# Both heads of an attention unit in one operation, and the state readout on four quarters of the TensorE array

## The chip, the cores and the metric

The kernel runs on one core of a Trainium2 chip. The metric is device time of one execution in microseconds (us); lower is better. The core has five engines with a queue each: TensorE (PE, matrix products; its weight loads are listed as PEld), VectorE (DVE), ScalarE (ACT), GpSimd (POOL) and SyncE (SP, which here only issues DMAs). PSUM, where TensorE writes, has eight banks; each holds 512 fp32 values in each of 128 partitions.

## The reference

Three layers follow each other. The first is a gated linear attention with a state, for 4 batches x 8 heads, 768 steps and 48 channels:

```python
for t in range(S):
    state = alpha[:, :, t, :, None] * state + np.einsum('bhd,bhe->bhde', k[:, :, t], v[:, :, t])
    y[:, :, t] = np.einsum('bhd,bhde->bhe', q[:, :, t], state)
```

The heads' outputs are put side by side to 3072 tokens of 384 channels. The second layer is `h = x @ w_in; g = h - tanh(h); x = g @ w_out` with 2048 hidden channels. The third routes each token to one of eight experts (the largest of eight logits) and weighs the expert's output by the softmax value and by a sigmoid output gate.

## The kernel before, in words

Tokens are worked in 8 blocks (`j`) of 384. The attention of one block is 4 units (`p`), each with two heads: head 0 in partitions 0 to 47, head 1 in partitions 64 to 111. So there are 32 units `u`. A unit's 384 steps are cut into `NC` = 6 chunks of `CH` = 64. For each unit the kernel

- scans the decays on DVE (`prep_k`, `prep_q1`) and scales keys and queries with them (`kh`, `kt`, and `prep_q2` for the queries: head 0 into `XA` on DVE, head 1 into `XB` on POOL);
- turns the keys (`turn_k`, TensorE transposes into a bank, `ktok` copied out by ACT) and computes each chunk's contribution to the state (`update`, after `carry` has put the state of the block before in front); a DVE scan, `chain`, makes of it the states `SS` at the start of all chunks, stored as 48 columns x 7 values, so that the states of one chunk lie 7 values (28 bytes) apart;
- multiplies keys and queries within a chunk (`score`) and masks the result (`causal`: one operation for each head's half, on DVE; in units 4 to 7, `CAU`, the second half goes by an ACT copy and a POOL product);
- copies the states on ACT (`states`) beside the values, so that `WA` has head 0's states in partitions 0 to 47 and its values in partitions 64 to 127, and `WB` the reverse for head 1; in the same way `XA` and `XB` have scaled queries and masked scores one below the other;
- reads out (`readout`): for each chunk one product over all 128 partitions for each head, head 0 to output partitions 0 to 63 and head 1 to 64 to 127, side by side in the array;
- copies the result (`y`, a high part by ACT and a low part by DVE in `place`) and lays it out by DMA as `xT`, the input of the second layer: 10 DMAs a block.

The second layer works in fp32r with high and low parts: each of 16 steps `f` of a block has 9 products into a bank of `psh` (`h_step`, first layer), `tanh` on ACT, subtraction on DVE, the high part `gg` by ACT and the low part by DVE or, in block 0, POOL; then 9 products into three accumulator banks `psx` (`x_step`, one step behind). An accumulator has 384 output columns and 16 router columns of its 512. In block 0 each step also narrows and splits the weights (`conv`: DVE L308 to L312, ACT copies, POOL subtractions) and runs `gate(f)`: three transposes of the step's output weights, a copy `wT` by ACT, products with the router weights, `ohi` by ACT and `olo` by DVE. Transposes and products of `gate` use one bank of `psa`.

The PSUM banks are: `psx` three, `psh` two, `psa` three. `psa` serves transposes of keys, state updates, scores, readouts, `gate` and the ranks of the router. In the first four units, before block 0, the `psx` banks help out (`bank`, `early`).

The order of the work: the first four units run ahead of block 0, in an order written out by hand. After that, a unit takes four steps of the second layer: scores, `carry` and `update` in the first, `chain` and `states` in the second, `readout` and `place` in the third, `turn_k` of the next unit in the fourth. In block 0 the order on DVE and SP is written by hand, and the other engines' order is planned from a time model; in blocks 1 to 6 the planner orders all, SP from block 2 on; the last block and the experts (third layer, from some 595 us on) are by hand again. Units end with block 6.

Of the kernel before, what the change touches and what calls it, by code (L numbers as in the profile page):

```python
# [9 lines left out]
F32 = mybir.dt.float32  # L10
# [26 lines left out]
CAU = (4, 5, 6, 7)  # L37
# [27 lines left out]
def tile_kernel(ctx, tc, aps, outs):  # L65
# [23 lines left out]
    psa = pss.enter_context(tc.tile_pool(name="psa", bufs=3, space=PSUM))  # L89
# [30 lines left out]
    XA = [ap1.tile([128, TB], F32, name=f"XA{i}") for i in range(2)]  # L120
    XB = [ap1.tile([128, TB], F32, name=f"XB{i}") for i in range(2)]
    WW = NC * D + 16
    WA = [ap1.tile([128, WW], F32, name=f"WA{i}") for i in range(2)]
    WB = [ap1.tile([128, WW], F32, name=f"WB{i}") for i in range(2)]
    GE = [ap1.tile([128, D, NC + 1], F32, name=f"GE{i}") for i in range(2)]
    VZ = [ap1.tile([128, NA, 2, 2 * D], F32, name=f"VZ{i}") for i in range(2)]
    SS = [ap1.tile([128, D, NC + 1], F32, name=f"SS{i}") for i in range(NP)]
# [64 lines left out]
    def prep_q2(u):  # L192
        s = st[u]
        q, Pc = s["raw"][:, TB:2 * TB], s["Pc"]
        yield dve.tensor_tensor(out=c3(XA[u % 2])[0:D], in0=c3(q)[0:D], in1=Pc[0:D, :, 1:CH + 1], op=ALU.mult)  # L195
        pool.tensor_tensor(out=c3(XB[u % 2])[64:64 + D], in0=c3(q)[64:64 + D], in1=Pc[64:64 + D, :, 1:CH + 1], op=ALU.mult)  # L196
# [19 lines left out]
    def score(u):  # L216
        s = st[u]
        s["sc"] = ps = bank("pss")
        for c in range(NC):
            cs = slice(c * CH, (c + 1) * CH)  # L220
            pe.matmul(ps[64:128, cs], s["kt"][0:D, c], XA[u % 2][0:D, cs], start=True, stop=True)  # L221
            pe.matmul(ps[0:64, cs], s["kt"][64:64 + D, c], XB[u % 2][64:64 + D, cs], start=True, stop=True)

    def causal(u):
        ps = st[u].pop("sc")
        for X, p0 in ((XA, 64), (XB, 0)):
            if p0 == 0 and u in CAU:
                act.copy(X[u % 2][p0:p0 + 64], ps[p0:p0 + 64, 0:TB])
                pool.tensor_tensor(out=c3(X[u % 2][p0:p0 + 64]), in0=c3(X[u % 2][p0:p0 + 64]),
                                   in1=cmask[p0:p0 + 64].unsqueeze(1).to_broadcast([64, NC, CH]), op=ALU.mult)  # L230
                continue
            yield dve.tensor_tensor(
                out=c3(X[u % 2][p0:p0 + 64]), in0=c3(ps[p0:p0 + 64, 0:TB]),
                in1=cmask[p0:p0 + 64].unsqueeze(1).to_broadcast([64, NC, CH]), op=ALU.mult)

    def carry(u):
# [5 lines left out]
        else:  # L242
            act.copy(pu[:, 0:n * D:n], SS[p][:, :, NC])
# [11 lines left out]
    def chain(u):  # L255
        yield dve.tensor_tensor_scan(  # L256
            out=SS[units[u][1]].rearrange("p d c -> p (d c)"), data0=GE[u % 2].rearrange("p d c -> p (d c)"),
            data1=st[u].pop("pu")[:, 0:(NC + 1) * D], initial=0.0, op0=ALU.mult, op1=ALU.add)
# [847 lines left out]
```

## Time and profile before

| | |
|---|---|
| median of 3 runs | 847.51 us (846.33 to 848.63) |
| profiled execution | 847.61 us, span 845.8 us |
| TensorE busy | 807.6 us (95%) |
| VectorE busy | 510.2 us (60%) |
| ScalarE busy | 384.3 us (45%) |
| GpSimd busy | 242.7 us (29%) |
| mean granted TensorE clock | 0.977 |

The span runs from the first to the last instruction of the profiled execution. Busy times are sums over the span. Products are pipelined, so a busy TensorE isn't one at its peak; what an engine waited for is inferred from semaphore events. The granted clock is TensorE's, as a share of 2.4 GHz.

### The profile page before, as it was taken

The numbers are of one execution on the slowest core, as the hardware profiler recorded it, in microseconds if no ns is written. First come the engines' busy times: TensorE is split into PE (matmuls) and PEld (weight loads), VectorE is DVE, ScalarE is ACT, GpSimd is POOL, SyncE is SP. The second block draws the span as 40 slices with busy tenths as digits, with TensorE's granted clock in tenths as the row PEclk, the third lists the DMA queues.
The fourth block names the chain that finished last, engine by engine and source line by source line (L and its number), as shares of the span: only waits on it lengthen the run. The fifth ranks groups of instructions, "written<-read, shape, count | busy, mean of one in ns | idle before, by whom it ended". The sixth has DMA issues, their size and how long they took to land.

```text
span 845.8 us, 15740 instructions
## 1 busy us (share of the span) xinstructions
PE 807.6 (95%) x5968; PEld 753.2 (89%) x5968; DVE 510.2 (60%) x1064; ACT 384.3 (45%) x803; POOL 242.7 (29%) x216
## 2 busy tenths in 40 slices
PE   6689889999999999999999999999999999999995
PEld 4578878999999989999999899999899999999995
DVE  8997989766766665766766664445443434434421
ACT  3555545544444445545443543435343434445431
POOL 6266766121211211120121020012223314424321
PEclk8799999999999999999999999999999999999998
DMA  9556552774322332232242221024345336235400
GB/s 253 156 179 199 170 162 57 232 245 104 90 61 70 94 92 58 76 116 65 64 127 64 58 69 24 15 98 126 130 147 202 103 116 217 96 109 205 156 25 30
DMA packets 59750, 98.48 MB, mean 116 GB/s; under 512 B 19724, under 2 KB 46113, under 8 KB 59665
## 3 DMA queue, kind: packets, MB, share of 16 engines
q1 hardware_dynamic: 56256, 87.91, 34.7%
q0 software_dynamic: 3408, 9.47, 2.9%
q8 instruction: 49, 0.80, 0.4%
q14 instruction: 37, 0.30, 0.1%
HBM read 72.13 MB, written 16.25 MB: 104 GB/s over the span
## 4 chain that ended last, share of the span: by engine, by line
PE 53%; DVE 19%; DMA 9%; issue 8%; ACT 6%; SPq 3%; POOL 2%; POOLq 0%; DVEq 0%; ACTq 0%
PE x L389 13%; PE psh L367 12%; PE o L861 11%; PE psf L833 10%; DMA raw<-raw 7%; DVE Ex L174 3%; DVE t L375 2%; DVE gg L378 2%; SPq L298 2%; DVE w L310 2%; DVE XA L195 2%; DVE w L308 1%; DVE SS L256 1%; PE pss L221 1%; ACT gg L377 1%
## 5 line engine op out<-in xcount | busy, mean ns | idle before, releaser
L389 PE MATMUL x<-ohi,gg 128*128 128x400 f32 x768 | 221.4, 357 | 4.8 <-POOL gg L378 1.3
L367 PE MATMUL psh<-xT,whi 128*128 128x384 f32 x768 | 204.6, 347 | 0.0
L389 PEld LDWEIGHTS x<-ohi,gg 128*128 128x128 f32 x768 | 138.6, 189 | 13.8 <-DVE gg L378 4.3
L367 PEld LDWEIGHTS psh<-xT,whi 128*128 128x128 f32 x768 | 139.7, 192 | 1.1 <-issue 0.3
L389 PE MATMUL x<-olo,gg 128*128 128x400 f32 x384 | 132.4, 345 | 0.0
L367 PE MATMUL psh<-xT,wlo 128*128 128x384 f32 x384 | 131.5, 342 | 0.0
L861 PE MATMUL o<-hi,hh 128*128 128x384 f32 (+2 forms) x440 | 115.1, 338 | 0.0
L375 DVE TENSOR_TENSOR t<-psh,t 128x384 f32<-128x384 f32 x128 | 70.5, 550 | 73.9 <-ACT t L373 73.1
L833 PE MATMUL psf<-xe,hi 128*128 128x256 f32 (+6 forms) x432 | 109.4, 338 | 0.0
L377 ACT CAST gg<-t 128x384 fp32r<-128x384 f32 x128 | 65.7, 513 | 78.6 <-DVE t L375 77.7
L373 ACT ACTIVATE t<-psh 128x384 f32<-128x384 f32 x128 | 62.2, 486 | 82.0 <-PE psh L367 81.2
L839 DVE SCALAR_TENSOR_TENSOR hh<-psf,hh 128x384 fp32r<-128x384 f32 (+3 forms) x96 | 40.9, 447 | 89.9 <-ACT hh L837 89.6
L378 DVE TENSOR_TENSOR gg<-t,gg 128x384 fp32r<-128x384 f32 x114 | 63.6, 557 | 36.0 <-ACT gg L377 35.6
L196 POOL TENSOR_TENSOR XB<-raw,P 48x384 f32<-48x384 f32 x32 | 34.5, 1079 | 160.8 <-issue 119.6
L861 PEld LDWEIGHTS o<-hi,hh 128*128 128x128 f32 (+2 forms) x440 | 78.2, 184 | 1.3 <-DVE hh L839 0.2
L833 PEld LDWEIGHTS psf<-xe,hi 128*128 128x128 f32 x432 | 75.8, 188 | 2.7 <-issue 0.3
L861 PE MATMUL o<-lo,hh 128*128 128x384 f32 (+1 forms) x232 | 77.7, 337 | 0.0
L837 ACT ACTIVATE hh<-psf 128x256 fp32r<-128x256 f32 (+6 forms) x72 | 34.9, 484 | 93.1 <-PE psf L833 75.2
L768 POOL TENSOR_TENSOR lo<-s,hi 128x768 fp32r<-128x768 f32 (+1 forms) x24 | 48.9, 2039 | 94.8 <-ACT hi L767 94.1
L367 PEld LDWEIGHTS psh<-xT,wlo 128*128 128x128 f32 x384 | 73.8, 192 | 0.0
L389 PEld LDWEIGHTS x<-olo,gg 128*128 128x128 f32 x384 | 72.4, 189 | 0.0
L833 PE MATMUL psf<-xe,lo 128*128 128x256 f32 (+6 forms) x216 | 71.9, 333 | 0.0
(147 smaller groups left out, 1274.6 us busy)
## 6 DMA issues: line engine op xcount, KB each, us to landing
raw<-raw SPq DMA_DIRECT2D x32, 579.5 KB, 4.1
wst<-wio SPq DMA_DIRECT2D x32, 384.0 KB, 4.0
s<-w SPq DMA_DIRECT2D x24, 512.0 KB, 4.1
s<-w SPq DMA_DIRECT2D x32, 384.0 KB, 5.1
xT<-y SPq DMA_DIRECT2D x48, 144.0 KB, 2.8
rows<-blank SPq DMA_DIRECT2D x8, 772.0 KB, 6.3
VZ<-vn SPq DMA_DIRECT2D x60, 72.0 KB, 2.4
xs<-rows SPq DMA_DIRECT2D x4, 772.0 KB, 7.3
```

Of the source, the lines that this page charges most:

```text
L196: pool.tensor_tensor(out=c3(XB[u % 2])[64:64 + D], in0=c3(q)[64:64 + D], in1=Pc[64:64 + D, :, 1:CH + 1], op=ALU.mult)
L367: pe.matmul(begun[f][:, 0:TB], w[:, kc, fs], xT[j][:, x, kc], start=(kc + n == 0), stop=(kc == KC - 1 and n == 2))
L373: act.activation(out=t, in_=ps[:, 0:TB], func=AF.Tanh)
L375: dve.tensor_tensor(out=g, in0=ps[:, 0:TB], in1=t, op=ALU.subtract)
L377: act.copy(gg[:, 0], g)
L378: (pool if j == 0 and f not in GLD else dve).tensor_tensor(out=gg[:, 1], in0=g, in1=gg[:, 0].bitcast(F32), op=ALU.subtract)
L389: pe.matmul(px[j][a][:, 0:DG], gg[:, gi, a * 128:(a + 1) * 128], w[:, f], start=(f == 0 and n == 0), stop=(f == NF - 1 and n == 2))
L768: (dve, pool)[i % 2].tensor_tensor(out=lo, in0=t, in1=hi.bitcast(F32), op=ALU.subtract)
L833: pe.matmul(ps[:, 0:n], w[:, kc, fs], xe[:, x, kc], start=(i == 0), stop=(i == 3 * KC - 1))
L837: act.activation(out=hh[:, 0:n], in_=ps[:, 0:n], func=AF.Relu)
L839: dve.scalar_tensor_tensor(out=hh[:, o:o + c.stop - c.start], in0=ps[:, c], scalar=0.0, in1=hh[:, c].bitcast(F32), op0=ALU.max, op1=ALU.su ...
L861: pe.matmul(po[q][m][0:p.stop - p.start, 0:DM], hh[:, p], w[:, f], start=(f == 0 and i == 0), stop=(f == NFE - 1 and i == len(parts) - 1))
```

## The change

- The query product, the mask and the scores are one operation for both heads: `X0` holds both heads' scaled queries, `X1` both heads' masked scores (rows 0 to 63 and 64 to 127). `XB` on POOL goes, and so does the split of `causal` (`CAU`).
- `states` goes: `readout` takes the states straight from `SS` as weights, 48 rows, one value in seven. The values have a tile of their own, `WV`, loaded by one DMA. For each chunk and head there are two products, states and values, that add up in PSUM. Chunks 0 to 2 go to output partitions 0 to 63, chunks 3 to 5 to 64 to 127; head 0 to one bank, head 1 to another. So four products in a row lie on four quarters of the array.
- A pair of banks, `psy`, replaces two of the three of `psa`. Readout uses the first half of each of the two banks, the scores of units 4 and later the second half; `psa` has one bank.
- `gate` puts its router products into free columns of the three accumulators. It runs a step ahead (`gate(f + 1)` in step `f`), and `olo` becomes `gate_low`, queued behind the subtraction of `h_step`. `start` is set so that the products and the accumulators share a bank, with their order on TensorE fixed by `issue_after`.
- `place` cuts each `xT` DMA into two, since the two halves of a block's steps now lie in different partitions.

```diff
-    psa = pss.enter_context(tc.tile_pool(name="psa", bufs=3, space=PSUM))
+    psy = pss.enter_context(tc.tile_pool(name="psy", bufs=1, space=PSUM))
+    psa = pss.enter_context(tc.tile_pool(name="psa", bufs=1, space=PSUM))
...
-    early = [(p, t) for i in range(3) for p, t in ((psx, f"x{i}"), (psa, "at"))] * 3
-    early = early[:4 * NP]
+    early = [(psx, "x0"), (psx, "x1"), (psx, "x2"), (psa, "at")] * 4
+    early = early[:3 * NP + 1]
...
+    def pair(name):
+        return psy.tile([128, 2, 512], F32, tag="py", name=name)
...
-        sp.dma_start(out=WA[u % 2][64:128, 0:NC * D], in_=aps["vw"][j, p, 64:128])
-        sp.dma_start(out=WB[u % 2][0:64, 0:NC * D], in_=aps["vw"][j, p, 0:64])
+        sp.dma_start(out=WV[u % 2][:, 0:NC * D], in_=aps["vw"][j, p])
...
-        yield dve.tensor_tensor(out=c3(XA[u % 2])[0:D], in0=c3(q)[0:D], in1=Pc[0:D, :, 1:CH + 1], op=ALU.mult)
-        pool.tensor_tensor(out=c3(XB[u % 2])[64:64 + D], in0=c3(q)[64:64 + D], in1=Pc[64:64 + D, :, 1:CH + 1], op=ALU.mult)
+        yield dve.tensor_tensor(out=c3(X0[u % 2]), in0=c3(s["raw"][:, TB:2 * TB]), in1=s["Pc"][:, :, 1:CH + 1], op=ALU.mult)
...
     def score(u):
         s = st[u]
-        s["sc"] = ps = bank("pss")
+        if u < NP:
+            ps = bank("pss")[:, 0:TB].rearrange("p (b t) -> p b t", b=2)
+        else:
+            s["py"] = pair("psy")
+            ps = s["py"][:, :, TB // 2:TB]
+        s["sc"] = ps
         for c in range(NC):
             cs = slice(c * CH, (c + 1) * CH)
-            pe.matmul(ps[64:128, cs], s["kt"][0:D, c], XA[u % 2][0:D, cs], start=True, stop=True)
-            pe.matmul(ps[0:64, cs], s["kt"][64:64 + D, c], XB[u % 2][64:64 + D, cs], start=True, stop=True)
+            o = ps[:, 2 * c // NC, c % (NC // 2) * CH:(c % (NC // 2) + 1) * CH]
+            pe.matmul(o[0:64], s["kt"][0:D, c], X0[u % 2][0:D, cs], start=True, stop=True)
+            pe.matmul(o[64:128], s["kt"][64:64 + D, c], X0[u % 2][64:64 + D, cs], start=True, stop=True)
...
+        b4 = [128, 2, NC // 2, CH]
+        yield dve.tensor_tensor(out=X1[u % 2].rearrange("p (b c t) -> p b c t", b=2, t=CH),
+                                in0=ps.rearrange("p b (c t) -> p b c t", t=CH),
+                                in1=cmask.unsqueeze(1).unsqueeze(1).to_broadcast(b4), op=ALU.mult)
...
-    def states(u):
-        SP = SS[units[u][1]]
-        act.copy(WA[u % 2][0:D, 0:NC * D].rearrange("p (c d) -> p c d", d=D), SP[0:D, :, 0:NC].rearrange("p d c -> p c d"))
-        act.copy(WB[u % 2][64:64 + D, 0:NC * D].rearrange("p (c d) -> p c d", d=D), SP[64:64 + D, :, 0:NC].rearrange("p d c -> p c d"))
...
-        ps = bank("psy")
-        for c in range(NC):
-            cs = slice(c * CH, (c + 1) * CH)
-            pe.matmul(ps[0:64, cs], WA[u % 2][:, c * D:c * D + 64], XA[u % 2][:, cs], start=True, stop=True)
-            pe.matmul(ps[64:128, cs], WB[u % 2][:, c * D:c * D + 64], XB[u % 2][:, cs], start=True, stop=True)
+        ps = s.pop("py") if u >= NP else pair("psy")
+        SP, h = SS[p], NC // 2
+        for c in range(h):
+            for x in range(2):
+                for q in range(2):
+                    for hh in range(2):
+                        cc = q * h + c
+                        cs = slice(cc * CH, (cc + 1) * CH)
+                        o = ps[64 * q:64 * q + 64, hh, c * CH:(c + 1) * CH]
+                        if x == 0:
+                            rs = slice(64 * hh, 64 * hh + D)
+                            w, m = SP[rs, :, cc], X0[u % 2][rs, cs]
+                        else:
+                            rs = slice(64 * hh, 64 * hh + CH)
+                            w, m = WV[u % 2][rs, cc * D:cc * D + 64], X1[u % 2][rs, cs]
+                        pe.matmul(o, w, m, start=(c + x == 0), stop=(x == 1), skip_group_check=True)
...
-                sp.dma_start(out=xT[j][c % 128:c % 128 + n, :, c // 128, :].bitcast(F32), in_=y[s0:s0 + n].bitcast(F32))
+                for q in range(2):
+                    s0 = 64 * q + c - c0
+                    sp.dma_start(out=xT[j][c % 128:c % 128 + n, :, c // 128, q * TB // 2:(q + 1) * TB // 2].bitcast(F32),
+                                 in_=y3[s0:s0 + n, :, hh].bitcast(F32))
...
-        for k in range(KC):
-            pe.matmul(ps[:, DM:DG], wT[:, k], wg[:, k], start=(k == 0), stop=(k == KC - 1))
-        act.copy(ohi[:, f, DM:DG], ps[:, DM:DG])
-        dve.tensor_tensor(out=olo[:, f, DM:DG], in0=ps[:, DM:DG], in1=ohi[:, f, DM:DG].bitcast(F32), op=ALU.subtract)
+        pl = px[0][f % NA][:, DG + f // NA * 2 * E:DG + (f // NA + 1) * 2 * E]
+        with tc.issue_after(px0[f % NA].ins) if f > 2 else ExitStack():
+            for k in range(KC):
+                i = pe.matmul(pl, wT[:, k], wg[:, k], start=(f < 3 and k == 0), stop=(k == KC - 1), skip_group_check=True)
+        if f == 2:
+            px0.append(i)
+        act.copy(ohi[:, f, DM:DG], pl)
+        gated[f] = pl
+
+    def gate_low(f):
+        dve.tensor_tensor(out=olo[:, f, DM:DG], in0=gated.pop(f), in1=ohi[:, f, DM:DG].bitcast(F32), op=ALU.subtract)
...
+        if j == f == 0:
+            with tc.issue_after(px0.pop().ins):
+                px0.extend(x_products(j, f, gg))
...
-            if f in gates and j == 0:
-                gate(f)
+            if j == 0:
+                for i in (f, f + 1):
+                    if i in gates:
+                        gate(i)
             gg = h_step(j, f)
+            for i in list(gated):
+                gate_low(i)
...
-            elif ph == 1 and live:
-                states(u)
```

## Rows read from the trace of the kernel before

**Rows 1.** Windows: stretch, its length, busy us (instructions) of each engine, clock, DMA

```profile
0.00:45.00 45.00, 30.89 (x321) 22.09 (x321) 40.03 (x78) 20.57 (x45) 21.43 (x36) 0.81 0.73 200
45.00:145.00 100.00, 89.65 (x670) 81.09 (x670) 88.98 (x159) 54.36 (x133) 70.64 (x60) 0.91 0.51 157
145.00:540.00 395.00, 391.74 (x3264) 364.52 (x3263) 254.86 (x559) 186.39 (x411) 63.68 (x63) 1.00 0.33 93
540.00:846.00 306.00, 295.35 (x1719) 285.53 (x1718) 126.30 (x270) 123.01 (x215) 86.98 (x59) 0.99 0.36 122
```

**Rows 2.** Waits of TensorE, 45 to 145 us: total us, times, longest

```profile
PE pst L212 <- DVE olo L352: 4.8, 3, 2.3
PE pso L346 <- DVE olo L352: 3.8, 2, 2.4
```

**Rows 3.** Waits of VectorE, 45 to 145 us

```profile
DVE olo L352 <- ACT ohi L351: 6.2, 7, 2.1
```

**Rows 4.** Timeline of TensorE, one readout: start us, duration us

```profile
303.03 0.27 PE L280 MATMUL psy<-XA,WA 128*64 128x64 f32 x1
...
303.14 0.22 PE L280 MATMUL psy<-XA,WA 128*64 128x64 f32 x1
...
303.72 0.22 PE L280 MATMUL psy<-XA,WA 128*64 128x64 f32 x1
303.73 0.22 PE L281 MATMUL psy<-XB,WB 128*64 128x64 f32 x1
```

**Rows 5.** Lines by form, TensorE: count, busy us, mean ns, idle before

```profile
L280 PE MATMUL psy<-XA,WA 128*64 128x64 f32 x384 | 34.5, 236 | 0.0
...
L252 PE MATMUL psu<-VZ,ktok 128*64 128x96 f32 x360 | 22.2, 255 | 1.5 <-ACT raw L205 1.2 <-issue 0.3
```

**Rows 6.** Lines by form, ScalarE

```profile
L262 ACT COPY WA<-SS 48x288 f32<-48x288 f32 x32 | 24.0, 751 | 31.6 <-DVE SS L256 31.5
...
L214 ACT COPY ktok<-pst 128x384 f32<-128x384 f32 x32 | 15.1, 473 | 12.8 <-PE pst L212 12.8
...
L351 ACT CAST ohi<-pso 128x16 fp32r<-128x16 f32 x16 | 2.7, 167 | 5.9 <-PE pso L350 5.9
```

**Rows 7.** Lines by form, TensorE's weight loads

```profile
L389 PEld LDWEIGHTS x<-ohi,gg 128*128 128x128 f32 x768 | 138.6, 189 | 13.8 <-DVE gg L378 4.3 <-ACT gg L377 2.4 <-POOL gg L378 1.6
...
L280 PEld LDWEIGHTS psy<-XA,WA 128*64 128x64 f32 x384 | 27.6, 144 | 8.2 <-issue 3.3 <-ACT r L427 1.3 <-ACT t L373 1.2
```

**Rows 8.** Lines by form, GpSimd

```profile
L196 POOL TENSOR_TENSOR XB<-raw,P 48x384 f32<-48x384 f32 x32 | 34.5, 1079 | 160.8 <-issue 119.6 <-PE psy L281 35.1 <-PE pso L350 2.5
...
L229 POOL TENSOR_TENSOR XB<-XB,cst 64x384 f32<-64x384 f32 x4 | 5.6, 1392 | 0.0
```

**Rows 9.** Instructions of two lines, VectorE: ns min/median/max, first and last start

```profile
L188 DVE TENSOR_SCALAR rP<-P x32: 158/172/985, 7.4 to 490.2; 128x6 f32<-128x6 f32 x32
...
L176 DVE TENSOR_TENSOR kh<-raw,Ex x32: 526/559/1086, 6.0 to 491.1; 128x384 f32<-128x384 f32 x32
```

**Rows 10.** Timeline of all engines near 58 us

```profile
58.31 1.06 POOL L196 TENSOR_TENSOR XB<-raw,P 48x384 f32<-48x384 f32 x1 [1.06 <-DVE P L184]
58.52 0.88 DVE L188 TENSOR_SCALAR rP<-P 128x6 f32<-128x6 f32 x1
```

**Rows 11.** Timeline of VectorE near 21 us

```profile
20.97 1.08 DVE L176 TENSOR_TENSOR kh<-raw,Ex 128x384 f32<-128x384 f32 x1
22.09 0.56 DVE L232 TENSOR_TENSOR XA<-pss,cst 64x384 f32<-64x384 f32 x1
22.68 0.55 DVE L232 TENSOR_TENSOR XB<-pss,cst 64x384 f32<-64x384 f32 x1
```

**Rows 12.** Timeline of GpSimd near 20 us

```profile
19.72 1.92 POOL L196 TENSOR_TENSOR XB<-raw,P 48x384 f32<-48x384 f32 x1
```

**Rows 13.** Instructions of line 298, SyncE's queue

```profile
L298 SPq DMA_DIRECT2D xT<-y x80: 595/645/1746, 23.7 to 536.8; - x80
```

**Rows 14.** Waits of SyncE's queue, 45 to 145 us

```profile
SPq L317 <- DVE w L312: 43.3, 13, 6.8
```

More of the change, by code (lines that the diff above doesn't have):

```diff
@@ L118, in tile_kernel @@
     olo = wp.tile([128, NF, DG], F32R, name="olo")
-    XA = [ap1.tile([128, TB], F32, name=f"XA{i}") for i in range(2)]
-    XB = [ap1.tile([128, TB], F32, name=f"XB{i}") for i in range(2)]
+    X0 = [ap1.tile([128, TB], F32, name=f"X0{i}") for i in range(2)]
+    X1 = [ap1.tile([128, TB], F32, name=f"X1{i}") for i in range(2)]
     WW = NC * D + 16
-    WA = [ap1.tile([128, WW], F32, name=f"WA{i}") for i in range(2)]
-    WB = [ap1.tile([128, WW], F32, name=f"WB{i}") for i in range(2)]
+    WV = [ap1.tile([128, WW], F32, name=f"WV{i}") for i in range(2)]
     GE = [ap1.tile([128, D, NC + 1], F32, name=f"GE{i}") for i in range(2)]
     VZ = [ap1.tile([128, NA, 2, 2 * D], F32, name=f"VZ{i}") for i in range(2)]
-    SS = [ap1.tile([128, D, NC + 1], F32, name=f"SS{i}") for i in range(NP)]
-    early = [(p, t) for i in range(3) for p, t in ((psx, f"x{i}"), (psa, "at"))] * 3
-    early = early[:4 * NP]
+    SS = [ap1.tile([128, 64, NC + 1], F32, name=f"SS{i}") for i in range(NP)]
+    early = [(psx, "x0"), (psx, "x1"), (psx, "x2"), (psa, "at")] * 4
+    early = early[:3 * NP + 1]
     def bank(name):
@@ L242, in carry @@
         else:
-            act.copy(pu[:, 0:n * D:n], SS[p][:, :, NC])
+            act.copy(pu[:, 0:n * D:n], SS[p][:, 0:D, NC])
     def update(u):
@@ L256, in chain @@
         yield dve.tensor_tensor_scan(
-            out=SS[units[u][1]].rearrange("p d c -> p (d c)"), data0=GE[u % 2].rearrange("p d c -> p (d c)"),
+            out=SS[units[u][1]][:, 0:D].rearrange("p d c -> p (d c)"), data0=GE[u % 2].rearrange("p d c -> p (d c)"),
             data1=st[u].pop("pu")[:, 0:(NC + 1) * D], initial=0.0, op0=ALU.mult, op1=ALU.add)
-    def states(u):
-        SP = SS[units[u][1]]
-        act.copy(WA[u % 2][0:D, 0:NC * D].rearrange("p (c d) -> p c d", d=D), SP[0:D, :, 0:NC].rearrange("p d c -> p c d"))
-        act.copy(WB[u % 2][64:64 + D, 0:NC * D].rearrange("p (c d) -> p c d", d=D), SP[64:64 + D, :, 0:NC].rearrange("p d c -> p c d"))
     def weave(*gens):
@@ L276, in readout @@
         s = st[u]
-        ps = bank("psy")
-        for c in range(NC):
-            cs = slice(c * CH, (c + 1) * CH)
-            pe.matmul(ps[0:64, cs], WA[u % 2][:, c * D:c * D + 64], XA[u % 2][:, cs], start=True, stop=True)
-            pe.matmul(ps[64:128, cs], WB[u % 2][:, c * D:c * D + 64], XB[u % 2][:, cs], start=True, stop=True)
+        ps = s.pop("py") if u >= NP else pair("psy")
[14 more added lines that the diff above has]
+                        pe.matmul(o, w, m, start=(c + x == 0), stop=(x == 1), skip_group_check=True)
         s["y"] = y = (g3.tile([128, 2, TB], F32R, tag="gg", name="y") if 0 < u < 4 else ap1.tile([128, 2, TB], F32R, tag="y", name="y"))
         s["py"] = ps
-        act.copy(y[:, 0], ps[:, 0:TB])
+        act.copy(y[:, 0].rearrange("p (b t) -> p b t", b=2), ps[:, :, 0:TB // 2])
     def place(u):
@@ L288, in place @@
         y, ps = st[u]["y"], st[u]["py"]
-        dve.tensor_tensor(out=y[:, 1], in0=ps[:, 0:TB], in1=y[:, 0].bitcast(F32), op=ALU.subtract)
+        y3 = y.rearrange("p s (b t) -> p s b t", b=2)
+        dve.tensor_tensor(out=y3[:, 1], in0=ps[:, :, 0:TB // 2], in1=y3[:, 0].bitcast(F32), op=ALU.subtract)
         if p == 0:
@@ L337, in conv @@
             load_w(n // 2, n % 2)
-    gates = {}
+    gates, gated = {}, {}
+    px, px0 = {}, []
     def gate(f):
@@ L379, in h_step, with x_products @@
         return gg
-    px = {}
     def x_step(j, f, gg):
-        if f == 0:
+        if f == 0 and j:
             px[j] = [psx.tile([128, 512], F32, tag=f"x{a}", name=f"x{a}") for a in range(NA)]
+        if j == f == 0:
+            with tc.issue_after(px0.pop().ins):
+                px0.extend(x_products(j, f, gg))
+        else:
+            x_products(j, f, gg)
+    def x_products(j, f, gg):
+        begin = []
         for a in range(NA):
@@ L388, in x_step @@
             for gi, w in ((0, ohi), (1, ohi), (0, olo)):
-                pe.matmul(px[j][a][:, 0:DG], gg[:, gi, a * 128:(a + 1) * 128], w[:, f],
+                i = pe.matmul(px[j][a][:, 0:DG], gg[:, gi, a * 128:(a + 1) * 128], w[:, f],
                           start=(f == 0 and n == 0), stop=(f == NF - 1 and n == 2))
+                if n == 0:
+                    begin.append(i)
                 n += 1
+        return begin
     def scores(pool_, r, n):
@@ L634, in tile_kernel @@
         pool.memset(VZ[i][0:64, :, 1], 0.0)
-        for X, p0 in ((XA, 32), (XB, 96)):
-            pool.memset(X[i][p0:p0 + 32], 0.0)
-        for W, p0 in ((WA, 32), (WB, 96)):
-            pool.memset(W[i][p0:p0 + 32, 0:NC * D], 0.0)
-            pool.memset(W[i][:, NC * D:WW], 0.0)
+        pool.memset(WV[i][:, NC * D:WW], 0.0)
+    for p in range(NP):
+        pool.memset(SS[p][:, D:64], 0.0)
     pool.memset(blank[:, 0:DM + 1], 0.0)
@@ L724, in tile_kernel @@
     dve.tensor_copy(base, cst[:, 368:376])
+    px[0] = [psx.tile([128, 512], F32, tag=f"x{a}", name=f"x{a}") for a in range(NA)]
     pend = None
@@ L1070, in layout @@
         vc = vt.reshape(NBLK, NP, NC, CH, D).transpose(0, 1, 3, 2, 4)
[L1071 removed]
+        vw[:, :, 64 * hh:64 * hh + 64] = vc
         vn = vt.reshape(NBLK, NP, NA, 128, D).transpose(0, 1, 3, 2, 4)
```

14 lines of the change are left out of this document (removed).

## The prediction

> **What bounds the kernel now.** I read the windows first, cut where the work changes [rows 1]. Four stages show. In the first 45 us VectorE is busy for 40.0 and TensorE for 30.9 at a mean granted clock of 0.81 (a mix of its two levels, 1.2 and 2.4 GHz): the first four units of attention, a chain through VectorE. From 45 to 145 us (block 0, with the weights being narrowed and split) VectorE is busy for 89.0 of 100 and TensorE for 89.7 at 0.91: both are near full and each waits for the other. From 145 to 540 us (blocks 1 to 6) TensorE is busy for 391.7 of 395 at full clock: only TensorE work can move that stage, and only 3.3 us of gaps are left in it. After 540 us no attention runs. So an edit is worth what it does to VectorE's chain in stage one, to the mutual waits in stage two, and to TensorE's own time in stage three.
>
> The second view is who waits for whom in stage two. TensorE stands 4.8 + 3.8 = 8.6 us before transposes (of `kh` and of gate weights), each time until VectorE's `olo` of the gate is done: `olo` reads the bank which the transposes want [rows 2]. VectorE in turn stands 6.2 us, seven times, because `olo` is queued ahead of the step's other work and waits for ScalarE's `ohi`, which waits for the router products [rows 3].
>
> **Part by part.**
>
> *Scores.* Still 12 products a unit, two at a time on opposite corners, each in two instructions with 64 columns. The two come out on other rows and over two banks; nothing in the rows prices that. I take 0.
>
> *Readout.* Before: 12 products a unit over 128 rows, in 12 pairs of instructions (`WA` and `WB` side by side). The first pair starts at 303.03, the last at 303.72: 0.70 us a unit, from 303.14 on 0.058 us a pair [rows 4]. After: 24 products over 48 or 64 rows, 48 instructions, four at a time: 12 groups of four. The trace shows two at a time, never four. Lower bound: a group takes what a pair takes, 0.058, so no change. Upper bound: the quarters run only in pairs, 24 x 0.058 = 1.40 us, +0.70 a unit. The nearest row is the pair: its two members start 0.01 us apart or less, so four starts fit in less than 0.058. I take 0.063 a group: 12 x 0.005 = +0.06 us a unit, over 24 units in stage three +1.4 us. The Trainium skill (TensorE: Matmul & The Clock Gate, Part 3) has the span of packed tiles grow by about 4 ns for each tile; by that the stage would be 24 x 12 x 8 ns = 2.3 us longer, an estimate from that page; no run here shows four.
>
> *Weights at a step.* The state half now loads its weights straight from `SS`, one value in seven (a step of 28 bytes); six of the 12 groups do. No row shows such a load. Lower bound: TensorE's update writes its output at this same step, and 96 columns take 255 ns against 236 for 64 [rows 5]: 19 ns for 32 columns, less than the 29 that the pair's pace gives, so the step costs nothing there. Upper bound: ScalarE reads the same `SS` at the same step in 751 ns for 288 values; from 473 for 384 and 167 for 16 (0.83 ns a value) 288 would take 393 [rows 6]: 1.9 times. The load has no spare time: 64 more columns lengthen it by 189 - 144 = 45 ns [rows 7], so 64 columns stream in about the time of a pair. At 1.9 times a group goes from 0.058 to 0.110: 6 x 0.052 = +0.31 us a unit, 7.5 us over 24. I take 0, since the first row is TensorE's own, but the other is close and gets a large chance. The Trainium skill (Advanced Engine Details and Errata, Memory Cachelines) says that an SBUF access that changes its 16-byte line every time pays a penalty; the ScalarE row agrees, with 751 against 393.
>
> *What ScalarE and GpSimd lose.* Both state copies go (751 and about as much, a unit), `XB` on GpSimd goes (1079), and in four units the copy of masked scores and GpSimd's product with the mask (1392) [rows 6, 8]. In stage three these lie beside TensorE; I give 0.9 us of the 3.3 us of gaps to them. In stage two they press on VectorE: a six-value operation takes 0.88 us beside `XB`, 0.17 in the median [rows 9, 10]. Four `XB` and four masks go, 4 x 1.08 + 4 x 1.39 = 9.9 us of GpSimd's 70.6. At 0.7 each that would be 5.6 us at most, 0 at least, for GpSimd's other 61 us still collide; I take 1.5.
>
> *Causal.* Two VectorE operations of 0.56 and 0.55 become one over all 128 rows. In stage one the second is on the chain, 22.68 after 22.09, and `kh` before it took 1.08 beside GpSimd's `XB` of 19.72 to 21.64, where 0.56 is its median [rows 9, 11, 12]. 0.55 + 0.5 for two units is 2.1. Against it stands the readout's pair of banks, of which there is one: a unit's readout waits for the subtraction of the unit before. I take -1.5 for stage one, between -3 and +2.
>
> *Router columns.* The gate's products leave the transposes' bank for free columns of the accumulators, `gate` runs one step ahead, and `olo` moves behind the step's subtraction. The 8.6 us of TensorE and the 6.2 us of VectorE were waits on exactly this. VectorE has 11 us idle in the stage and TensorE 10 [rows 1]; closing 6.2 on VectorE shortens the stage by at most that. Next late is GpSimd's low half of `gg` and the narrowing, so I take 4. With the 1.5 stage two gives -5.5; bounds -12 and +2. The added wait: ScalarE's and VectorE's reads of these columns and TensorE's accumulation share a bank, so a third of each step's products stands behind `olo`; queued behind them on TensorE are the next step's first-layer products, and VectorE's subtraction waits for those.
>
> *One bank less twice.* `psa` falls from three banks to one: transposes of `kh`, state update, gate transposes and ranks follow each other in it. A unit has some 16 us for two such holds; I take 0, at most +0.3 us a unit, 7 us.
>
> *SyncE.* The `vw` load becomes one, but each `xT` piece becomes two: +80 issues at 645 ns, 52 us over the kernel [rows 13], three more a unit at most. In stage two SyncE stands 43.3 us for VectorE's narrowing anyway [rows 14], which covers them; without cover +2 us a unit there, 8 us. The last two units of stage one add five issues, which delay the first layer of block 0 by 3.2 us; TensorE has 14 us to spare there [rows 1]. I take 0.
>
> **Sum.** Profiled execution: 847.6 (span 845.8). Stage one -1.5, stage two -5.5, stage three +1.4 - 0.9 = +0.5, last stage 0: 841.1. The median of the runs shown is 847.5, so 841.0.
>
> **Rivals.**
> *Slow weight loads.* The step of 28 bytes halves the loads' pace: +7.5 in stage three, where nothing hides it: 848.5. For it speaks the ScalarE row, against it the update's. In stages one and two the product is not alone in setting the end, so I add nothing there.
> *The quarters take turns.* Loads or products of two quarters in the same columns exclude each other, so readout takes 1.40 us a unit. 0.70 x 24 = 16.8 in stage three: 857.9, slower. It decides as soon as a group of four takes over 0.082 us: then 12 x 0.024 x 24 = 7 us eat the gain of the first stages. Against it: pairs beside each other run at full pace; for it: no row has two products over different rows of the same columns.
> *The wait moves.* In block 0 the accumulators' products wait for `olo` as the transposes did: TensorE's 8.6 us come back before the products, stage two gains nothing: 846.6. For it: VectorE's step ends late, after the narrowing; against it: only one bank in three is held, and TensorE can run the first layer ahead.
>
> **How the numbers follow.** Forecast 0.42, slow loads 0.28, turns 0.14, moved wait 0.16. A measurement of this kernel can't tell less than 0.3%, 2.5 us, from no change, so faster means below 845.0 and slower above 850.1. The forecast is faster in 0.92 of its cases (its own range 835 to 846), slow loads in 0.1, the moved wait in 0.25; slower are all turns, a quarter of slow loads, 0.15 of the moved wait. Faster: 0.39 + 0.03 + 0.04, some 0.45; slower: 0.14 + 0.07 + 0.02, some 0.24; the rest 0.31. The range reaches from a stage two that gains its full 11 or 12 us to the readout in turns: 834 to 858.
>
> **What would show it.** Right: readout groups start some 0.06 us apart, a unit's readout stays at 0.70 to 0.78 us; no wait of TensorE on `olo`; stage two is some 94 us long, stage three 395 or 396. Slow loads: groups 0.11 us apart for state weights, 0.06 for `WV`. Turns: 0.11 or more for all. Moved wait: TensorE's waits name `olo` before the accumulators' products. The prediction is wrong if stage two does not shrink or stage three grows by more than 4 us.

## The result, and the profile after

The kernel after takes 857.19 us (median of 4 runs, 855.71 to 859.21) against 847.51: ratio 1.0116, 95% interval [1.0089, 1.0143]. It is slower, and the forecast of 841.0 was wrong in its direction; the range (834 to 858) held the median. The profiled execution, the longest of the four, took 859.21 us (span 857.4), so its span is 11.6 us longer than before's 845.8, where the medians are 9.7 us apart.

Where did the 11.6 us go? First the windows of the kernel after, cut as in [rows 1] (length, busy us and instructions of each engine, granted clock, DMA).

```profile
0.00:45.00 45.00, 31.16 (x428) 22.68 (x430) 36.89 (x75) 14.87 (x37) 11.79 (x25) 0.81 0.69 200
45.00:145.00 100.00, 88.30 (x709) 77.03 (x705) 76.80 (x142) 40.39 (x107) 47.37 (x44) 0.88 0.47 148
145.00:540.00 395.00, 394.17 (x3787) 369.86 (x3786) 234.05 (x545) 159.10 (x371) 42.78 (x48) 1.00 0.32 94
540.00:858.00 318.00, 306.64 (x1822) 296.21 (x1820) 129.51 (x276) 126.06 (x221) 86.95 (x59) 0.99 0.34 118
```

In the second stretch VectorE is busy for 12 us less than in [rows 1] (76.80 against 88.98), and less of block 0 gets done: the stretch became idler, not shorter. In the third TensorE has 0.8 us of gaps left. Windows cut at fixed times hide a shift, so I follow one event through both kernels: VectorE's subtraction `t` of a step of the first layer, 16 steps to a block. Its timeline in the kernel before, steps 0, 1, 15, 31 and 112:

```profile
48.27 0.55 DVE L375 TENSOR_TENSOR t<-psh,t 128x384 f32<-128x384 f32 x1
...
55.78 0.55 DVE L375 TENSOR_TENSOR t<-psh,t 128x384 f32<-128x384 f32 x1
...
143.04 0.54 DVE L375 TENSOR_TENSOR t<-psh,t 128x384 f32<-128x384 f32 x1
...
209.46 0.56 DVE L375 TENSOR_TENSOR t<-psh,t 128x384 f32<-128x384 f32 x1 [0.34 <-ACT t L373]
...
542.24 0.56 DVE L375 TENSOR_TENSOR t<-psh,t 128x384 f32<-128x384 f32 x1 [1.52 <-ACT t L373]
```

and the same steps in the kernel after:

```profile
45.95 0.55 DVE L398 TENSOR_TENSOR t<-psh,t 128x384 f32<-128x384 f32 x1
...
58.47 0.55 DVE L398 TENSOR_TENSOR t<-psh,t 128x384 f32<-128x384 f32 x1
...
152.46 0.55 DVE L398 TENSOR_TENSOR t<-psh,t 128x384 f32<-128x384 f32 x1
...
218.15 0.55 DVE L398 TENSOR_TENSOR t<-psh,t 128x384 f32<-128x384 f32 x1
...
553.82 0.56 DVE L398 TENSOR_TENSOR t<-psh,t 128x384 f32<-128x384 f32 x1 [2.04 <-ACT t L396]
```

The differences, in us: up to step 0, -2.3 (stage one, gained); step 0 to 1, 12.5 against 7.5, +5.0; steps 1 to 15, 94.0 against 87.3, +6.7; steps 15 to 31 (block 1), -0.7; steps 31 to 112 (blocks 2 to 6, 20 units of attention), 335.7 against 332.8, +2.9. That makes the 11.6. The three losses have three places and, in the main, three causes.

**The first step.** VectorE in the kernel after, from the first subtraction on (start, duration, and in brackets the idle time before and what ended it):

```profile
45.95 0.55 DVE L398 TENSOR_TENSOR t<-psh,t 128x384 f32<-128x384 f32 x1
46.42 0.17 DVE L375 TENSOR_TENSOR olo<-x,ohi 128x16 fp32r<-128x16 f32 x1
53.43 0.17 DVE L375 TENSOR_TENSOR olo<-x,ohi 128x16 fp32r<-128x16 f32 x1 [6.84 <-ACT ohi L371]
53.52 0.55 DVE L234 TENSOR_TENSOR X<-psy,cst 128x384 f32<-128x384 f32 x1
```

and TensorE in the same stretch:

```profile
48.33 0.52 PE L390 MATMUL psh<-xT,wlo 128*128 128x384 f32 x1
48.65 3.79 PE L677 MATMUL warm<-ones,oneb 128*128 128x384 bf16 x12
52.14 0.48 PE L390 MATMUL psh<-xT,whi 128*128 128x384 f32 x1
52.45 0.74 PE L368 MATMUL x<-wg,wT 128*128 128x16 f32 x6
53.12 0.72 PE L254 MATMUL psu<-VZ,ktok 128*64 128x96 f32 x12
```

VectorE's second `olo` is that of the next step's gate. Its six products stand on TensorE behind the 12 products that only keep that engine busy. Everything else that VectorE has for this step is queued behind this `olo`.

**The rest of block 0.** VectorE's waits, 45 to 145 us, which answer to [rows 3] (6.2 us there), and then TensorE's, which answer to [rows 2]:

```profile
DVE olo L375 <- ACT ohi L371: 19.6, 11, 6.8
DVE SS L258 <- PE psu L254: 3.6, 3, 1.3
```

```profile
PE pso L361 <- DVE w L326: 7.5, 6, 2.0
PE psh L390 <- DVE olo L375: 2.1, 2, 1.2
PE psh L390 <- DVE t L398: 2.1, 2, 1.2
```

The waits of transposes on `olo` are gone, as forecast. In their place TensorE stands 7.5 us before the gate's transposes until VectorE has narrowed the weights `w`, since a gate a step ahead asks for them earlier (in the runs below, 9.0 us with the router part alone, none with each gate in its own step): together with the 2.1 us on `olo` that is more than the 8.6 us before. VectorE's wait at `olo` has tripled, and it has a new one, of the state chain for the update. Step 4 shows both, with TensorE's update in the last row:

```profile
77.42 0.55 DVE L398 TENSOR_TENSOR t<-psh,t 128x384 f32<-128x384 f32 x1
80.20 0.17 DVE L375 TENSOR_TENSOR olo<-x,ohi 128x16 fp32r<-128x16 f32 x1 [2.23 <-ACT ohi L371]
80.29 0.55 DVE L234 TENSOR_TENSOR X<-psy,cst 128x384 f32<-128x384 f32 x1
82.15 0.85 DVE L258 TENSOR_TENSOR_SCAN SS<-GE,psu 128x336 f32<-128x336 f32 x1 [1.31 <-PE psu L254]
...
81.38 0.72 PE L254 MATMUL psu<-VZ,ktok 128*64 128x96 f32 x12
```

**The readout.** One of them in the kernel after (each row is four products, eight instructions), against [rows 4]:

```profile
313.08 0.42 PE L292 MATMUL psy<-X,SS 48*64 48x64 f32 x8
313.31 0.30 PE L292 MATMUL psy<-X,WV 64*64 64x64 f32 x8
313.43 0.42 PE L292 MATMUL psy<-X,SS 48*64 48x64 f32 x8
313.67 0.30 PE L292 MATMUL psy<-X,WV 64*64 64x64 f32 x8
```

After a row with `SS` the next starts 0.23 us later, after one with `WV` 0.12: 0.117 and 0.06 a group of four instructions. The weight loads say why (ns min/median/max, 145 to 540 us):

```profile
L292 PEld LDWEIGHTS psy<-X,SS x552: 187/204/215, 159.5 to 529.3; 48*64 48x64 f32 x184
L292 PEld LDWEIGHTS psy<-X,WV x552: 129/133/153, 159.7 to 529.5; 64*64 64x64 f32 x184
```

### The profile page after: what moved, and what is told of

Read it like the earlier page. It is cut to its first block, busy times and chain, and to the rows that moved or that the text cites. A ratio compares the mean times of both kernels' runs of the same rounds, so it can differ in the third digit from the quotient of the medians.

```text
span 857.4 us, 17117 instructions
## 1 busy us (share of the span) xinstructions
PE 820.3 (96%) x6736; PEld 765.8 (89%) x6736; DVE 477.2 (56%) x1036; ACT 340.4 (40%) x735; POOL 188.9 (22%) x174
## 4 chain that ended last, share of the span: by engine, by line
PE 80%; DVE 8%; issue 6%; DMA 3%; SPq 1%; ACT 1%; POOL 1%; POOLq 0%; DVEq 0%; ACTq 0%
PE x L418 23%; PE psh L390 23%; PE o L891 11%; PE psf L863 11%; PE psy L292 4%; PE psy L228 2%; PE psu L254 2%; DVE Ex L176 1%; DVE w L324 1%; DVE w L322 1%; SPq L311 1%; PE pst L842 1%; PE pst L212 1%; DMA raw<-raw 1%; DVE w L326 1%
## 5 line engine op out<-in xcount | busy, mean ns | idle before, releaser
L418 PE MATMUL x<-ohi,gg 128*128 128x400 f32 x768 | 218.2, 358 | 0.5
L390 PE MATMUL psh<-xT,whi 128*128 128x384 f32 x768 | 207.8, 347 | 7.4 <-DMA xT<-y 2.9
L390 PEld LDWEIGHTS psh<-xT,whi 128*128 128x128 f32 x768 | 142.2, 193 | 10.4 <-DMA xT<-y 2.8
L400 ACT CAST gg<-t 128x384 fp32r<-128x384 f32 x128 | 65.8, 514 | 68.3 <-DVE t L398 65.7
L192 POOL TENSOR_TENSOR kt<-kh,rP 128x384 f32<-128x384 f32 x32 | 28.4, 887 | 273.0 <-PE psy L229 245.7
```

The costliest lines, as they stand in the source:

```text
L390: pe.matmul(begun[f][:, 0:TB], w[:, kc, fs], xT[j][:, x, kc], start=(kc + n == 0), stop=(kc == KC - 1 and n == 2))
L400: act.copy(gg[:, 0], g)
L418: i = pe.matmul(px[j][a][:, 0:DG], gg[:, gi, a * 128:(a + 1) * 128], w[:, f], start=(f == 0 and n == 0), stop=(f == NF - 1 and n == 2))
```

## The experiments

Three theories came out of this: A, VectorE's written order (`olo` ahead of its time); B, the one bank that is left for transposes, gates and updates; C, the step of the state weights. After the first run a theory F came in, the fill products ahead of the gate. All ratios are against the kernel before on the same chip.

**`olo` in its own step.**

```diff
             for i in list(gated):
-                gate_low(i)
+                if i <= f:
+                    gate_low(i)
```

> The kernel after, with one change: VectorE takes the low half of a step's router columns (olo) in that step, as before, and not a step ahead; the products of the gate still run a step ahead in the accumulators' banks. Theory A (VectorE's written order): the 9.5 us that block 0 lost are VectorE standing 19.9 us at olo for ScalarE's ohi of the step after, with the masking, the state chain and the narrowing queued behind. Then VectorE's waits at olo fall from 19.9 us to under 4, block 0 gives back 7 to 10 us, and the time is 847 to 851. Theory B (one bank): transposes of kh and of gate weights, the carried state and the update follow each other in the one bank that is left, and TensorE waits for its holder; olo only shows it. Then block 0 stays within 2 us, and the time is 855 to 858.

Measured: 865.29, 1.0195 [1.0169, 1.0222]. Both expectations missed; it is 7 to 8 us slower than after, in the profiled run 4.7 of them in block 1, which no run explains. VectorE's waits in block 0:

```profile
DVE SS L258 <- PE psu L254: 19.9, 4, 6.5
DVE olo L375 <- PE x L418: 6.6, 4, 2.2
```

The wait at `olo` fell from 19.6 to 6.6 us, and the same 20 us stand one instruction further on, at the state chain. The first step still takes 12.1 us. Theory A falls: `olo` was where VectorE stood, not why.

**Contiguous state weights.**

```diff
+    def states(u):
+        act.copy(SC[u % 2], SS[units[u][1]][:, :, 0:NC].rearrange("p d c -> p c d"))
...
-    w, m = SP[rs, :, cc], X0[u % 2][rs, cs]
+    w, m = (SC[u % 2][rs, cc] if u >= NP else SP[rs, :, cc]), X0[u % 2][rs, cs]
...
+            elif ph == 1 and live:
+                states(u)
```

> The kernel after, with one change: from the fifth unit on ScalarE copies a unit's states into a contiguous tile, and the readout loads its state weights from there instead of from every seventh value. Theory C (step of the weights): groups with state weights fall from 0.118 us to the 0.058 of the others, a unit's readout from 1.07 to about 0.71 us, and blocks 1 to 6, which TensorE bounds, lose 0.28 to 0.37 us a unit: 6 to 9 us, so 848 to 851, if the copies (some 0.8 to 1.0 us of ScalarE a unit) are hidden. Rival D (four quarters): the slow groups are slow because two of their four products have only 48 rows or because four products start at once; the copy then changes nothing in the groups, and the time is 856 to 859.

Measured: 853.51, 1.0065 [1.0047, 1.0083]. Its loads and one readout:

```profile
L296 PEld LDWEIGHTS psy<-X,SC x567: 129/133/135, 159.6 to 540.0; 48*64 48x64 f32 x189
```

```profile
311.19 0.30 PE L296 MATMUL psy<-X,SC 48*64 48x64 f32 x8
311.31 0.30 PE L296 MATMUL psy<-X,WV 64*64 64x64 f32 x8
311.42 0.30 PE L296 MATMUL psy<-X,SC 48*64 48x64 f32 x8
311.54 0.30 PE L296 MATMUL psy<-X,WV 64*64 64x64 f32 x8
```

Still 48 rows, still four products at a time, and every group at 0.06 us: the step of 28 bytes is the price (C), not the quarters (D). Steps 31 to 112 took 330.9 us against 335.7. The total came out 2.5 us above the expected 848 to 851. In the profiled run the first subtraction came 1.6 us later than in after, and TensorE's gaps in steps 31 to 112 grew from 0.9 to 4.0 us: it stands 3.8 us there for transfers of `xT` (0.7 in after, none before).

**The router part alone, in the kernel before.** The edits to `gate`, `x_step` and the step loop as in the change; attention and banks untouched.

> The kernel before, with only the router part of the change: gate products into free columns of the accumulators' banks, a step ahead, olo behind the step's subtraction; three banks for transposes and the rest, attention as before. Theory A: VectorE's new wait comes with this part alone, whatever the banks: block 0 is 5 to 10 us longer than before, 852 to 858. Theory B: with three banks nothing queues up, the waits of TensorE for olo (4.8 and 3.8 us before) go, and block 0 is as long as before or up to 5 us shorter: 842 to 848.

Measured: 852.52, 1.0057 [1.0036, 1.0079]. The first step takes 12.4 us, steps 1 to 15 take 87.2, as before. So the loss of the first step comes with the router part, and the 6.7 us that follow do not. Each theory was right for half of it; the total fits A (852 to 858) and misses B (842 to 848).

**One bank for everything, in the kernel before.**

```diff
-psa = ...tile_pool(name="psa", bufs=3, space=PSUM)
+psa = ...tile_pool(name="psa", bufs=1, space=PSUM)
...
```

The first four units keep six banks, by a pool of two more that only they use.

> The kernel before, with only the banks of the change: one bank instead of three for the transposes, scores, updates and readouts after stage one (the first four units keep their six banks). Scores and readouts share that one bank too here, which the kernel after does not ask, so this is an upper bound of the banks' price. Theory B: block 0 alone is 6 to 10 us longer, and all in all 854 to 862. Theory A: block 0 changes by less than 3 us; blocks 1 to 6 may pay some 0.3 us a unit, so 847 to 856.

Measured: 947.47, 1.1176 [1.1133, 1.1219], far above either expectation: block 0 some 27 us longer in steps 1 to 15, and 66 us in steps 31 to 112. It asks more of the bank than the change does, so it only says that banks are dear here.

**Without the last 12 fill products.**

```diff
     weave(prep_q(NP))
-    fill(12)
```

> The kernel after without the last 12 of the products that only keep TensorE busy (the loads and products of ones ahead of block 0). In the first step of block 0 VectorE stands from 46.5 to 53.4 us for the gate of the second step, whose products come on TensorE behind these 12, which take 3.8 us at half clock. The first run (olo a step later) moved the wait from olo to the state chain and left the 5 us, so the queue on TensorE is the suspect, not olo. Theory F (fills ahead of the gate): step one of block 0 is 3 to 4 us earlier, the time 853 to 855. Rival G (clock): without them TensorE's clock is half for longer, the products behind take twice as long, and the time is 856 to 860.

Measured: 854.86, 1.0088 [1.0068, 1.0108]. The first step takes 8.4 us, 4.1 less than after, and the total falls by 2.3, within the 853 to 855 of theory F: the gate no longer stands behind the fills.

**Each gate in its own step, one bank.**

```diff
-                for i in (f, f + 1):
+                for i in ((1, 2) if f == 1 else (f,)):
                     if i in gates:
                         gate(i)
```

with `olo` held back as in the first experiment.

> The kernel after with each gate in its own step instead of a step ahead (gates 0; then 1 and 2; then 3, 4 and so on), and olo in that step behind the subtraction. Theory F: the first step needs one gate, which is ready, so the 5 us of the first step go, and the time is 850 to 853. Theory B (one bank for update, gate and transposes) says that the further 6.6 us between steps 4 and 15 stay, since gate and update still follow each other in the bank. Rival H (the gate's place decides all): with both losses gone 844 to 848. Rival A: VectorE again stands at the gate of its own step, 856 or more.

Measured: 861.05, 1.0133 [1.0070, 1.0197] (four runs from 853.9 to 865.5): not to be told from after, and outside the 850 to 853 of theory F. The first step falls to 10.3 us, but steps 1 to 15 stay at 95.1, as B has it, block 1 is 5.0 us longer (as in the first experiment), and VectorE, in block 0, now stands 13.6 us before the narrowing, whose tile the gate's transposes hold while they wait for their turn.

**Each gate in its own step, in the kernel before.** The router part alone, with the same edit.

> The kernel before with the router columns in the accumulators' banks (as in the run of the router part alone, 1.0057 of before, which lost 5 us in the first step and nothing in the rest of block 0), but each gate in its own step. Theory F: the first step's loss goes, 846 to 849. Rival: the loss hangs on the accumulators' banks and not on the step ahead, 851 to 854.

Measured: 848.56, 1.0009 [0.9999, 1.0019], within the 846 to 849 of F. The first step takes 9.6 us, 2.8 less than a step ahead; beside the 2.1 that remain against before the trace shows another wait, 2.9 us of VectorE for a transfer of `raw`. But the router columns, now with three banks and no step ahead, gain nothing: steps 1 to 15 take 89.7 us, 2.4 more than before. TensorE's waits, 45 to 145 us:

```profile
PE psh L375 <- DVE olo L360: 6.0, 3, 2.6
PE x L403 <- DVE olo L360: 4.4, 3, 2.0
```

10.4 us on `olo`, where [rows 2] had 8.6: here the wait moved from the transposes to the products.

**The change's banks, in the kernel before.**

```diff
+psb = ...tile_pool(name="psb", bufs=2, space=PSUM)
-psa = ...tile_pool(name="psa", bufs=3, space=PSUM)
+psa = ...tile_pool(name="psa", bufs=1, space=PSUM)
...
-p, tag = early.pop(0) if early else (psa, "at")
+p, tag = early.pop(0) if early else ((psb, "sy") if name in ("pss", "psy") else (psa, "at"))
```

> The kernel before with the banks dealt as after: scores and readouts have two banks of their own, and transposes of kh, updates, gates and ranks share one instead of three. Attention, gate and router columns as before. Theory B: in each unit of block 0 the update waits on TensorE until the gate has left the bank, and VectorE's state chain waits for the update; 1.5 to 2.5 us a unit, so 5 to 9 us over block 0, 852 to 857. Rival: the order of the holders costs nothing, and the 6.6 us come from the attention itself: 846 to 849.

Measured: 874.19, 1.0334 [1.0296, 1.0372]. The mechanism of B, at some three times the price expected: steps 1 to 15 take 105.4 us, and the first step takes 13.6, though here each gate runs in its own step. VectorE's waits, 45 to 145 us, name the bank's holders in turn:

```profile
DVE olo L353 <- ACT ohi L352: 11.5, 5, 4.6
DVE w L309 <- PE pso L347: 11.0, 4, 3.2
DVE SS L257 <- PE psu L253: 7.5, 3, 5.7
```

With the router columns in that bank as well each gate holds it longer; the kernel after, with the columns elsewhere (and another attention), loses 6.7 us in steps 1 to 15 where this one loses 18.

**Three banks in the kernel after.** One pool of three, scores in one bank, a unit's readout in two tiles of it.

```diff
-psy = ...tile_pool(name="psy", bufs=1, space=PSUM)
-psa = ...tile_pool(name="psa", bufs=1, space=PSUM)
+psa = ...tile_pool(name="psa", bufs=3, space=PSUM)
...
-        return psy.tile([128, 2, 512], F32, tag="py", name=name)
+        return [bank(name), bank(name)]
```

> The kernel after with the banks dealt as before: one pool of three banks for transposes of kh, scores, updates, readouts, gates and ranks; a unit's readout takes two of them as two tiles, so its eviction and its subtraction are two instructions each with half the columns. Attention of both heads at once, the gate a step ahead and its columns are as after. Theory B (one bank): the 6.6 us that the kernel after loses between steps 4 and 15 of block 0 are the bank's, and go; the 5 us of the first step and the readout's 0.28 us a unit stay: 849 to 853. Rival I (the attention in one operation costs block 0 its time, as fewer and longer instructions on VectorE): nothing changes or it is slower by the halved instructions, 856 to 860.

Measured: 852.50, 1.0049 [1.0029, 1.0069], within the 849 to 853 of B. Steps 1 to 15 take 85.9 us: the 6.7 are gone, and 1.4 more. VectorE at step 4, against the rows of after above, and the first half of the update:

```profile
76.71 0.55 DVE L394 TENSOR_TENSOR t<-psh,t 128x384 f32<-128x384 f32 x1
77.44 0.17 DVE L371 TENSOR_TENSOR olo<-x,ohi 128x16 fp32r<-128x16 f32 x1 [0.18 <-ACT ohi L367]
77.53 0.55 DVE L228 TENSOR_TENSOR X<-pss,cst 128x384 f32<-128x384 f32 x1
77.99 0.84 DVE L252 TENSOR_TENSOR_SCAN SS<-GE,psu 128x336 f32<-128x336 f32 x1
...
74.27 0.55 PE L248 MATMUL psu<-VZ,ktok 128*64 128x96 f32 x6
```

From the subtraction to the end of the chain it takes 2.1 us instead of 5.6. The update starts 2.4 us ahead of the subtraction, in after 4.0 us behind it and behind the gate's products. The first step (11.8) and steps 31 to 112 (336.0) keep their losses. But block 1 takes 68.5 us against 65.7 in after: TensorE stands 1.9 us there for a transfer of `xT`, and its granted clock is 0.77 from 144.86 to 160 us. So of the 8.1 us by which steps 1 to 15 are shorter than in after, 5.2 are left at step 31, and the time is 4.7 us less.

**The parts together.** Three kernels combine the edits shown: three banks with contiguous weights and without fills; three banks with contiguous weights and each gate in its own step; and contiguous weights without fills with the change's own banks.

> The run with three shared banks, and with it the contiguous state weights (0.9957 of after alone) and without the last 12 fill products (0.9972 of after alone). If the three causes are independent, the parts add up: 857.2 - 6.6 - 3.7 - 2.4 = 844.5, so 842 to 848, about as before or faster. If they hide each other (a wait removed in one place comes back in the next, as in the first run), 849 to 853.

Measured: 844.45, 0.9955 [0.9937, 0.9972], where the sum of the parts gave 844.5.

> Three shared banks and contiguous state weights, and each gate in its own step with olo behind the subtraction; the fill products stay. In the kernel before this place of the gate was worth 4.0 us against a step ahead (848.6 against 852.5), in the kernel after, with one bank, nothing (861.1 against 857.2). Theory B: with three banks it is worth the 4 us again, and the time is 857.2 - 6.6 - 3.7 - 4.0 = 843, so 841 to 847. Rival: the gate's place costs what it did with one bank, 850 to 856.

Measured: 840.83, 0.9925 [0.9907, 0.9942]: faster than both kernels, the fastest here, and just below the expected 841 to 847.

> The kernel after with its own banks, contiguous state weights, and without the last 12 fill products. The two act in different stages (blocks 1 to 6 and the first step), so they add up: 857.2 - 3.7 - 2.4 = 851, 849 to 853, still slower than before by the bank's 6.6 us less what the attention gains. If one hides the other: 853 to 855.

Measured: 848.30, 1.0022 [1.0005, 1.0039], a little better than the sum (851) and than its range.

The table gathers the lengths between the same subtractions, in us.

| kernel | step 0 to 1 | steps 1 to 15 | steps 15 to 31 | steps 31 to 112 |
|---|---|---|---|---|
| before | 7.5 | 87.3 | 66.4 | 332.8 |
| after | 12.5 | 94.0 | 65.7 | 335.7 |
| before, router part alone | 12.4 | 87.2 | 68.3 | 332.6 |
| before, router part, own step | 9.6 | 89.7 | 65.2 | 332.9 |
| before, the change's banks | 13.6 | 105.4 | 68.3 | 331.6 |
| after, `olo` in its own step | 12.1 | 96.1 | 70.4 | 336.4 |
| after, gate and `olo` in their own step | 10.3 | 95.1 | 70.7 | 335.5 |
| after, no fill | 8.4 | 93.1 | 65.7 | 335.0 |
| after, contiguous weights | 11.8 | 93.2 | 65.6 | 330.9 |
| after, three banks | 11.8 | 85.9 | 68.5 | 336.0 |
| three banks, contiguous, no fill | 10.1 | 86.6 | 67.9 | 329.9 |
| three banks, contiguous, own step | 8.6 | 85.2 | 67.0 | 328.6 |
| after, contiguous, no fill | 8.0 | 92.2 | 65.8 | 328.4 |

In the main the first column follows the gate's place and the fills, the second the banks, the last the step of the weights. They are not wholly independent: without fills the first step takes 8.0 or 8.4 us with the change's banks and 10.1 with three, the kernel before with the change's banks loses 6.1 us in its first step, and part of what three banks give in block 0 is lost again in block 1.

## Why the prediction was wrong, step by step

*"One bank less twice ... I take 0."* This step failed, and it is the largest term: 6.7 us in block 0 (8.1 against the same kernel with three banks, 5.2 with block 1, and 4.7 in the time). I counted two holds of the bank in a unit's 16 us, which fits blocks 1 to 6. In block 0 there are four gates more in a unit, and with each the bank goes from TensorE to ScalarE and back. The update comes behind the gate, VectorE's chain waits for the update, and VectorE's order is written out, so all that follows waits too.

*"Router columns ... so I take 4."* Failed twice. In the first step a gate a step ahead stands behind work that was already queued: 5.0 us lost where I had named the queues behind the wait but not the queue ahead of the products that end it. And the gain did not come: the router part alone, with each gate in its own step, is 1.0009 of before, and TensorE's waits for `olo` only change place (10.4 us against 8.6). That was my rival of the moved wait; it holds, though not in the kernel after, where TensorE's wait on `olo` is down to 2.1 us; there TensorE waits 7.5 us for the narrowing instead, and VectorE 19.6 for `ohi`. What the columns may be good for is the one bank: the kernel before with the same banks and the columns left in it loses 18 us and not 6.7, though its attention differs too.

*"Weights at a step ... I take 0."* Wrong, and the rival of slow loads right: 0.117 us a group against the 0.110 that it gave, so 3 x 0.115 = 0.35 us a unit (rival 0.31) and 8.3 us over 24 units. TensorE's busy time shows it too: in steps 31 to 112 it is 334.8 us in after and 327.0 with the states copied, 7.8 us for 20 units. The Trainium skill (Advanced Engine Details and Errata, Memory Cachelines), weighed and not followed, speaks of a penalty for an access that leaves its line with each value; the trace agrees, with loads of 204 ns against 133. I had read the price of a step off the update's output [rows 5]. It did not carry over: loading weights at this step has a price that the update's writes do not show.

*What ScalarE and GpSimd lose.* I gave 0.9 us of stage three to them. The slow loads show as only 2.9 us in steps 31 to 112, because something else was gained there: TensorE is busy for 5.2 us more than before (334.8 against 329.5), but its gaps fall from 3.3 to 0.9 us. The gaps may be what ScalarE and GpSimd had cost, for before TensorE waited 2.5 us there for `gg` from VectorE and ScalarE, and in after it doesn't; no run tests it. With contiguous weights those steps take 328.4 to 330.9 us against 332.8, though one copy of the states is back; 2.6 us of that gain are TensorE's own busy time (327.0 against 329.5), which no run explains.

*Readout, scores, causal.* Right. Four quarters run side by side, at 0.06 us a group where the loads are contiguous (I took 0.063); the turns did not happen. Stage one gained 2.3 us (I took 1.5): the last subtraction of its four units came at 33.37 against 35.99, and 1.7 us of VectorE's lead then went to a wait for a weight transfer at 42 us. Block 0 with three banks is 0.6 to 2.1 us faster than before in steps 1 to 15, about the 1.5 that I gave to GpSimd's relief, but no run tests that relief alone, and block 1 is 0.6 to 2.1 us slower.

*SyncE, "I take 0".* Open. TensorE does not stand for a transfer of `xT` in the kernel before; in after it does for 2.9 us, 2.2 of them ahead of block 0, and in the other kernels with the change's attention for 1.4 to 6.2. Whether the doubled issues cause it was not tried; kernels without them can have it too (1.5 us in the router part alone, 1.6 with the change's banks).

*The sum.* Stage two: -5.5 forecast, +11.7 measured (5.0 and 6.7). Stage three: +0.5 forecast, +2.2 measured (-0.7 and 2.9). That the range held the median is luck: its upper end stood for a readout in turns, which did not happen. So is it that the kernel with the two failed steps repaired and the states copied took 840.83, near the 841.0 that I gave for the change as it was: against before its profiled run gained 2.8 us up to the first subtraction and 4.2 in steps 31 to 112, but only 0.4 in blocks 0 and 1 together, where I had put 5.5 into block 0 alone. What stays open is how much of the 6.7 us is the bank itself and how much the place that the planner of TensorE's order gives to the update because of it. At step 4 of after ScalarE has taken the gate's transposes out of the bank at 77.96 us and put the carried state in by 78.93; the update starts at 81.38, so 2.4 of its delay are TensorE's order. An order written out by hand was not tried.

## What to carry to other kernels

When a change gives up buffers, count the holds in the busiest stage, not in the longest one, and follow each hold through every engine that hands it on. When an instruction on a hand-ordered engine is to run a step earlier, look up what is already queued ahead of its producers; taking away the wait where it shows may only move it to the next instruction, as in the first experiment. A step in an operand has a price by the kind of access, so price it from a row of that same kind.

## What the runs showed of the hardware

The price of the step by access: weight loads of 64 columns take 204 ns at a step of 28 bytes and 133 without; the update's products, which write at this step, take 246 ns in the median, in both kernels. Their 12 instructions of 96 columns start 0.043 us apart (0.72 us in all), where the second layer's of 384 columns, written without a step, start 0.175 apart: about the same time for a column. No run writes the update without the step.

The fills cost more in the kernel after: 3.79 us for the 12, at a granted clock of 0.55, against 2.49 at 0.85 before. Windows of the kernel after around them (columns as in the first fence):

```profile
40.00:46.50 6.50, 3.45 (x30) 2.84 (x30) 4.81 (x11) 1.97 (x6) 2.13 (x3) 0.64 0.84 282
46.50:48.60 2.10, 2.04 (x6) 1.78 (x6) 0.09 (x2) 0.97 (x3) 2.10 (x3) 0.50 1.01 402
48.65:52.44 3.79, 3.79 (x14) 2.02 (x14) 0.00 (x0) 0.00 (x0) 0.48 (x1) 0.55 0.62 242
```

TensorE had stood idle for 2.25 us, from 39.69 to 41.94, for a transfer of `xT`:

```profile
41.94 1.01 PE L390 MATMUL psh<-xT,whi 128*128 128x384 f32 x2 [2.25 <-DMA xT<-y]
```

From there to 52 us the clock stood at 0.50, the lower of its two levels (1.2 of 2.4 GHz), and most of the fills ran at that: 1.3 us of the first step's loss. Before, TensorE was idle for 2.4 us up to 48.50, the clock was 0.50 behind it too, but only up to 51.6 us and 1.00 from 52, so that fewer of the fills, which started at 51.09, met it.
